# Weight pieces, output buffers and load order at the start of an attention and SwiGLU kernel

**Chip, cores, metric.** One core of one Trainium2 chip. The metric is the time of one execution on the device in microseconds (us). Where a ratio is quoted, it is the mean time of one kernel's fast runs over that of the other's fast runs of the same rounds, so not quite the ratio of the medians beside it.

## The reference

Softmax attention over 8 batches of 12 heads, 448 positions of 64 values; then the rows of all heads together (3584 x 768) go through a SwiGLU block of width 1536.

```
scores = q @ k^T / 8;  attn = softmax(scores);  x = (attn @ v)      # (8, 12, 448, 64)
x = x.transpose(0, 2, 1, 3).reshape(3584, 768)
g = x @ w_gate;  h = g * sigmoid(g) * (x @ w_val);  out = h @ w_out # (3584, 768) float32
```

## The kernel before

It works on pairs of heads. For each pair, TensorE turns q and k (`tp`) or, from pair 11 on, a DMA does; then come the scores `s`, the exponentials `E` on ScalarE, their sums and `pv` (tile `acc`). From pair 6 on, TensorE mixes the SwiGLU work of finished batches into the attention: `gp` and `vp` (gate and value, twelve column blocks each), then `op` (output). Until the first `gp` there is no SwiGLU work, and ScalarE's exponentials set the pace.

All loads of q, k, v and weights, except q and k of pair 0, are cast to 16 bits on the way. They go through one queue that GpSimd fills in program order. The parts that the change touches:

```python
WSPL = [(0, 384), (384, 384), (768, 768)]        # column pieces of gate and value
...
def load_w(kind, i): ...                          # each piece in two transfers, even and odd row pairs
...
def ffn2_steps(kk, c0, n, hts, first, last_block):        # op; first: block 0
    chunks = range(n // 128)
    if first:
        steps = [(ch, oh) for oh in range(2) for ch in chunks]    # all left halves, then all right
    else:
        steps = [(ch, oh) for ch in chunks for oh in range(2)]
    for ch, oh in steps:
        last = first or (last_block and ch == n // 128 - 1)
        if last or oh == 0:
            osb = fp.tile([128, DM], FP32, tag="osb", bufs=3)     # block 0: six tiles, half used
        ...                                       # 12 op matmuls into op
        nc.scalar.activation(osb[:, ds(m0, w)], op[:, 0:w], AF.Copy, scale=1.0 / HS)
        if not last:
            m0, w = 0, DM
            if oh == 0:
                continue                          # store whole chunks, except in block 0
        ...                                       # nc.sync.dma_start(out[...], osb[...])
...
load_qk16(1, 1); load_qk16(2, 1); load_qk16(3, 1)
load_v(0)                                         # v of pairs 0 to 2
load_qk16(4)                                      # q and k of pairs 4 and 5
load_v(1)
...
wq = {                                            # loads issued while pair number ... runs
    0: [("qk", 6), ("g", 0), ("v", 0)],
    1: [("qk", 8), ("g", 1), ("v", 1)],
    3: [("qk", 10), ("V", 2), ("g", 2), ("v", 2)],
    4: [("qk", 12)],
    6: [("V", 3), ("o", 0)],
    7: [("o", 1)],
}
```

The stores of the output and the DMA transposes share SyncE's queue, which is in order. Piece 2 of the value weights, used from column block 6 on, is called "value 2" below.

The softmax here doesn't subtract the row's maximum and nothing guards it: scores larger than these inputs give would overflow.

Of the kernel before, what the change touches and what calls it, by code (L numbers as in the profile page):

```python
# [10 lines left out]
FP32 = mybir.dt.float32  # L11
FP16 = mybir.dt.float16
# [15 lines left out]
def kernel(  # L28
# [10 lines left out]
    nc = tc.nc  # L39
    B, H, S, D = q.shape  # L40
    DM = H * D
    DF = moe_w_gate.shape[1]
    P = 112
    NC = S // P
    NCB = DM // 128
# [22 lines left out]
    consts = ctx.enter_context(tc.tile_pool(name="consts", bufs=1))  # L68
# [5 lines left out]
    fp = ctx.enter_context(tc.tile_pool(name="fp", bufs=3))  # L74
# [4 lines left out]
    ones = consts.tile([P, 32], FP16, name="ones")  # L79
    warm = consts.tile([128, 512], FP16, name="warm")  # L80
    ident = consts.tile([P, P], FP16, name="ident")
    WSPL = [(0, 384), (384, 384), (768, 768)]
    wgv = {}
    for kind in "gv":
        for i, (m0, m) in enumerate(WSPL):
            wgv[kind, i] = consts.tile([128, NCB, m], FP16, name=f"w{kind}{i}")

    def wslice(kind, fb, cb):
        i = min(fb // 3, 2)
        return wgv[kind, i][:, cb, ds(fb * 128 - WSPL[i][0], 128)]  # L90

    wo = [consts.tile([128, NFB, OH], FP16, name=f"wo{i}") for i in range(2)]

# [19 lines left out]
    def load_qk16(pr, n=2):  # L113
        q16 = raws.tile([P, 4, NC, D], FP16, tag="rq", bufs=RB, name="q16")
        k16 = raws.tile([P, 4, NC, D], FP16, tag="rk", bufs=RB, name="k16")
        for dst, src in ((q16, q), (k16, k)):
            flat = src.rearrange("b h s d -> (b h) s d")[2 * pr : 2 * pr + 2 * n]
            nc.gpsimd.dma_start(dst[:, 0 : 2 * n], flat.rearrange("h (p c) d -> p h (c d)", c=NC))
        for i in range(n):
            raw[pr + i] = (q16[:, 2 * i : 2 * i + 2], k16[:, 2 * i : 2 * i + 2])  # L120

    def load_v(g, lo=0, hi=2 * GP):
        b = g // GPB
        h0 = (g % GPB) * 2 * GP
        if lo == 0:
            v16[g] = raws.tile([P, 2 * GP, NC, D], FP16, tag="vt", bufs=3, name="vt")
        nc.gpsimd.dma_start(  # L127
            v16[g][:, lo:hi],
            v[b, h0 + lo : h0 + hi].rearrange("h (p c) d -> p h (c d)", c=NC),
        )  # L130

    def load_w(kind, i):
        if kind == "o":
            src = moe_w_out[:, ts(i, OH)].rearrange("(f p) m -> p f m", p=128)
            dst = wo[i]
        else:
            src = (moe_w_gate if kind == "g" else moe_w_val)[:, ds(*WSPL[i])].rearrange(
                "(a p t) m -> t p a m", p=128, t=2
            )
            for t in range(2):  # L140
                nc.gpsimd.dma_start(wgv[kind, i][:, t::2, :], src[t])
            return
        nc.gpsimd.dma_start(dst[:], src)
# [116 lines left out]
    def mm(dst, lhsT, rhs, start, stop):  # L260
        if not tiled[0]:
            nc.tensor.matmul(dst, lhsT=lhsT, rhs=rhs, start=start, stop=stop)  # L262
            return
        for j in range(4):
            nc.tensor.matmul(  # L265
                dst[ts(j, 32), :], lhsT=lhsT[:, ts(j, 32)], rhs=rhs, start=start, stop=stop
            )

    def ffn1_steps(kk, c0, n, hts):
        for fb in range(NFB):  # L270
            gp = ps_f.tile([128, 512], FP32, tag="f")
            for cb in range(NCB):
                mm(
                    gp[:, 0:n],
                    lhsT=wslice("g", fb, cb),
                    rhs=X[kk][:, cb, ds(c0, n)],
                    start=(cb == 0),
                    stop=(cb == NCB - 1),
                )
            sg = fp.tile([128, 512], FP32, tag="sg")  # L280
            nc.scalar.activation(sg[:, 0:n], gp[:, 0:n], AF.Tanh, scale=0.5)  # L281
            yield NCB * n / 2400.0
            vp = ps_f.tile([128, 512], FP32, tag="f")
            for cb in range(NCB):
                mm(
                    vp[:, 0:n],
                    lhsT=wslice("v", fb, cb),
                    rhs=X[kk][:, cb, ds(c0, n)],
                    start=(cb == 0),
                    stop=(cb == NCB - 1),  # L290
                )
            t1 = fp.tile([128, 512], FP32, tag="t1")
            nc.vector.scalar_tensor_tensor(  # L293
                t1[:, 0:n], sg[:, 0:n], 1.0, gp[:, 0:n], ALU.add, ALU.mult
            )
            nc.vector.scalar_tensor_tensor(  # L296
                hts[:, fb, 0:n], t1[:, 0:n], 0.5 * HS, vp[:, 0:n], ALU.mult, ALU.mult
            )
            yield NCB * n / 2400.0

    def ffn2_steps(kk, c0, n, hts, first, last_block):
        chunks = range(n // 128)
        if first:
            steps = [(ch, oh) for oh in range(2) for ch in chunks]
        else:
            steps = [(ch, oh) for ch in chunks for oh in range(2)]
        for ch, oh in steps:
            last = first or (last_block and ch == n // 128 - 1)
            if last or oh == 0:
                osb = fp.tile([128, DM], FP32, tag="osb", bufs=3)  # L310
            parts = [(oh * OH, OH)]
            if last_block and last and oh:
                parts = [(OH, OH // 2), (OH + OH // 2, OH // 2)]
            for m0, w in parts:
                op = ps_f.tile([128, 512], FP32, tag="f")
                for fb in range(NFB):
                    mm(
                        op[:, 0:w],
                        lhsT=hts[:, fb, ts(ch, 128)],
                        rhs=wo[oh][:, fb, ds(m0 - oh * OH, w)],  # L320
                        start=(fb == 0),
                        stop=(fb == NFB - 1),
# [5 lines that stand above are left out]
                        continue  # L328
                l0 = c0 + ch * 128
                l = l0  # L330
                while l < l0 + 128:
                    b, j = divmod(l, S)
                    c, p0 = divmod(j, P)
                    m = min(P - p0, l0 + 128 - l)
                    eng = nc.scalar if last_block and last and m < 64 else nc.sync
                    eng.dma_start(
                        out[ts(NB * kk + b, S), :].rearrange("(p c) m -> c p m", c=NC)[
                            c, p0 : p0 + m, ds(m0, w)
                        ],
                        osb[l - l0 : l - l0 + m, ds(m0, w)],  # L340
                    )
                    l += m
            yield NFB * OH / 2400.0

    def block(i):
        kk, odd = divmod(i, 2)
        c0, n = (384, 512) if odd else (0, 384)
        hts = hp_.tile([128, NFB, 512], FP16, tag="h")
        return ffn1_steps(kk, c0, n, hts), ffn2_steps(kk, c0, n, hts, i == 0, i == B - 1), n

    with tc.manual_schedule():
# [4 lines left out]
        make_identity(nc, ident)  # L356
        load_qk16(2, 1)
        load_qk16(3, 1)
        load_v(0)
        load_qk16(4)  # L360
        load_v(1)
        dummy(6)
        prep(0)()
# [4 lines left out]
            0: [("qk", 6), ("g", 0), ("v", 0)],  # L368
            1: [("qk", 8), ("g", 1), ("v", 1)],
            3: [("qk", 10), ("V", 2), ("g", 2), ("v", 2)],  # L370
            4: [("qk", 12)],
            6: [("V", 3), ("o", 0)],
            7: [("o", 1)],
        }
# [1 line left out]
        def emit(item):  # L376
            if item[0] == "qk":
                load_qk16(*item[1:])
            elif item[0] == "V":
                load_v(item[1])  # L380
            else:
                load_w(*item)
# [152 lines left out]
```

## Time and profile before

| | before |
|---|---|
| time, median of three runs (range) | 467.75 us (465.63 to 468.91) |
| span of the profiled run | 466.1 us |
| TensorE busy | 453.2 us, 97% |
| TensorE idle before 95 us, from 95 to 400, after 400 | 7.7, 0, 5 us |
| TensorE's wait for wv (the value weights) | 1.6 us |
| ScalarE's two waits for output stores in block 0 | 5.1 us together |

How to read it: TensorE has no hole for 305 us, so only what happens in the first 95 us and at the very end can move the time. The lines themselves stand in the prediction.

### The profile page before, as it was taken

How to read it: one execution, taken by the hardware profiler on the slowest of the kernel's cores; microseconds unless marked ns; L12 is line 12 of the kernel's file. 1: busy time of each engine (PE TensorE's matmuls, PEld its weight loads, DVE VectorE, ACT ScalarE, POOL GpSimd, SP SyncE). 2: the span in 40 equal slices, each digit the busy share in tenths (PEclk: the TensorE clock that was granted, in tenths of full speed). 3: DMA queues.
4: the chain of work that ended last, by engine and by line, in shares of the span. 5: the costliest groups of instructions: out<-in, count | busy, mean ns of one | idle time of the engine just before them, and what ended most of it. 6: DMA issues, size and time to landing. Idle time of an engine off the chain costs nothing.

```text
span 466.1 us, 14143 instructions
## 1 busy us (share of the span) xinstructions
PE 453.2 (97%) x6367; PEld 228.0 (49%) x6367; DVE 237.0 (51%) x371; ACT 242.9 (52%) x353; POOL 101.0 (22%) x160
## 2 busy tenths in 40 slices
PE   8799899999999999999999999999999999999995
PEld 3344444344455555444455555544445556555453
DVE  2665664366764553655545644636555546434310
ACT  7886555656565555545555565555555552222221
POOL 9454406331350042302223040210200000000000
PEclk9999999999999999999999999999999999999999
DMA  9999999991994383771948574913602111110123
GB/s 132 194 200 208 192 181 196 203 151 24 110 129 57 65 114 53 117 106 18 135 45 107 90 118 86 123 23 75 97 10 55 37 37 35 36 35 1 35 69 101
DMA packets 80925, 44.24 MB, mean 95 GB/s; under 512 B 36704, under 2 KB 77792, under 8 KB 80864
## 3 DMA queue, kind: packets, MB, share of 16 engines
q0 software_dynamic: 40768, 23.37, 38.6%
q1 hardware_dynamic: 40000, 19.92, 23.6%
q8 instruction: 50, 0.82, 0.7%
q14 instruction: 11, 0.09, 0.1%
q10 hardware_dynamic: 96, 0.05, 0.0%
HBM read 47.19 MB, written 11.01 MB: 125 GB/s over the span
## 4 chain that ended last, share of the span: by engine, by line
PE 80%; DMA 15%; POOL 2%; issue 1%; ACT 0%; SPq 0%; POOLq 0%; ACTq 0%
PE gp L265 14%; PE vp L265 12%; PE op L262 11%; PE op L265 10%; DMA q<-in_q_dram 9%; PE vp L262 9%; PE s L197 7%; PE acc L213 7%; PE gp L262 7%; PE acc L235 3%; DMA wg<-in_moe_w_gate_dram 3%; DMA k<-in_k_dram 2%; DMA out_dram<-osb 2%; POOL vt L127 0%; POOL qk L155 0%
## 5 line engine op out<-in xcount | busy, mean ns | idle before, releaser
L204 ACT ACTIVATE E<-s 112x896 f16<-112x896 f32 x192 | 164.8, 918 | 25.3 <-PE s L197 25.1
L281 ACT ACTIVATE sg<-gp 128x384 f32<-128x384 f32 (+1 forms) x96 | 52.3, 545 | 86.8 <-PE gp L265 54.2
L293 DVE SCALAR_TENSOR_TENSOR t<-sg,gp 128x384 f32<-128x384 f32 (+1 forms) x96 | 58.5, 610 | 64.9 <-ACT sg L281 64.8
L324 ACT ACTIVATE osb<-op 128x384 f32<-128x384 f32 (+1 forms) x57 | 27.7, 486 | 102.6 <-PE op L262 53.2
L265 PE MATMUL gp<-X,wg 128*32 128x512 f16 (+1 forms) x1416 | 78.1, 355 | 0.0
L250 DVE RECIPROCAL R<-ssb 128x112 f32<-128x112 f32 x92 | 73.1, 827 | 0.7
L296 DVE SCALAR_TENSOR_TENSOR hts<-t,vp 128x384 f16<-128x384 f32 (+1 forms) x96 | 59.6, 621 | 24.9 <-PE vp L262 8.4
L262 PE MATMUL op<-wo,hts 128*128 128x384 f16 (+1 forms) x408 | 68.6, 322 | 0.0
L265 PE MATMUL vp<-X,wv 128*32 128x512 f16 (+1 forms) x1224 | 66.9, 353 | 0.0
L227 DVE TENSOR_TENSOR X<-acc,R 128x448 f16<-128x448 f32 x48 | 29.7, 624 | 65.8 <-PE acc L213 64.0
L262 PE MATMUL vp<-X,wv 128*128 128x384 f16 (+1 forms) x270 | 58.6, 353 | 1.6 <-DMA wv<-in_moe_w_val_dram 1.6
L197 PE MATMUL s<-qkT 64*128 64x448 f16 x384 | 55.1, 355 | 3.4 <-ACT E L204 3.1
L262 PEld LDWEIGHTS <-hts 128*128 128x128 f16 x408 | 38.9, 98 | 28.2 <-issue 3.0
L265 PEld LDWEIGHTS <-wg 128*32 128x32 f16 x1416 | 37.8, 97 | 29.6
L265 PE MATMUL op<-wo,hts 128*32 128x384 f16 x1104 | 48.9, 326 | 0.0
L262 PE MATMUL gp<-X,wg 128*128 128x384 f16 (+1 forms) x222 | 47.4, 350 | 0.0
L265 PEld LDWEIGHTS <-wv 128*32 128x32 f16 x1224 | 32.7, 97 | 25.5
L213 PE MATMUL acc<-E,vt 112*32 112x448 f16 x768 | 45.2, 355 | 0.0
L127 POOL DMA_DIRECT2D vt<-in_v_dram x16 | 12.4, 774 | 148.1 <-PE acc L213 146.3
L262 PEld LDWEIGHTS <-wv 128*128 128x128 f16 x270 | 25.2, 98 | 28.6 <-issue 4.6
L265 PEld LDWEIGHTS <-hts 128*32 128x32 f16 x1104 | 29.5, 97 | 16.4
L155 POOL COPY qk<-q 112x512 f16<-112x512 f16 x37 | 22.9, 620 | 65.0 <-DMA qkT<-qk 46.2
(38 smaller groups left out, 198.6 us busy)
## 6 DMA issues: line engine op xcount, KB each, us to landing
vt<-in_v_dram POOLq DMA_DIRECT2D x16, 336.0 KB, 5.4
q<-in_q_dram POOLq DMA_DIRECT2D x22, 224.0 KB, 6.1
k<-in_k_dram POOLq DMA_DIRECT2D x22, 224.0 KB, 8.1
wo<-in_moe_w_out_dram POOLq DMA_DIRECT2D x2, 1152.0 KB, 26.1
out_dram<-osb SPq DMA_DIRECT2D x7, 288.0 KB, 2.8
out_dram<-osb SPq DMA_DIRECT2D x6, 336.0 KB, 2.9
out_dram<-osb SPq DMA_DIRECT2D x7, 240.0 KB, 2.7
out_dram<-osb SPq DMA_DIRECT2D x8, 192.0 KB, 2.7
```

The costliest lines, as they stand in the source:

```text
L155: nc.gpsimd.tensor_copy(dst, src)
L197: nc.tensor.matmul(s[:, hx, 0:S], lhsT=t[ts(hx, 64)].rearrange("p c q -> p (c q)")[:, c * P : c * P + 128], rhs=t[ts(hx, 64), NC:, :].rear ...
L204: nc.scalar.activation(E[pr][:, c], s[0:P, :, 0:S], AF.Exp, scale=sm_scale)
L213: nc.tensor.matmul(acc[ts(j, 32), 0:S], lhsT=v16[g][:, 2 * r + j % 2, c, :].rearrange("p (d t) -> p t d", t=2)[:, t], rhs=E[p0 + j // 2][: ...
L227: nc.vector.tensor_tensor(X[kk][:, hp + t, ts(bb, S)], acc[:, 0:S], R[p0][:], ALU.mult)
L250: lambda i=i: nc.vector.reciprocal(rt[:, ts(i, P)], ssb[:, ts(i, P)]) for i in range(4)
L262: nc.tensor.matmul(dst, lhsT=lhsT, rhs=rhs, start=start, stop=stop)
L265: nc.tensor.matmul(dst[ts(j, 32), :], lhsT=lhsT[:, ts(j, 32)], rhs=rhs, start=start, stop=stop)
L281: nc.scalar.activation(sg[:, 0:n], gp[:, 0:n], AF.Tanh, scale=0.5)
L293: nc.vector.scalar_tensor_tensor(t1[:, 0:n], sg[:, 0:n], 1.0, gp[:, 0:n], ALU.add, ALU.mult)
L296: nc.vector.scalar_tensor_tensor(hts[:, fb, 0:n], t1[:, 0:n], 0.5 * HS, vp[:, 0:n], ALU.mult, ALU.mult)
L324: nc.scalar.activation(osb[:, ds(m0, w)], op[:, 0:w], AF.Copy, scale=1.0 / HS)
```

## The change

Three intents: let the weights of column block 6 arrive sooner by moving fewer bytes ahead of them; give each output chunk of block 0 its own buffer for both halves, so that no eviction waits for a store; and have q and k of pairs 4 and 5 arrive sooner.

```diff
-    WSPL = [(0, 384), (384, 384), (768, 768)]
...
-        for i, (m0, m) in enumerate(WSPL):
-            wgv[kind, i] = consts.tile([128, NCB, m], FP16, name=f"w{kind}{i}")
+        for i in range(4):
+            wgv[kind, i] = consts.tile([128, NCB, DF // 4], FP16, name=f"w{kind}{i}")
...                                               (wslice and load_w follow suit)
+        osbs = {}
         for ch, oh in steps:
-            last = first or (last_block and ch == n // 128 - 1)
+            last = last_block and ch == n // 128 - 1
             if last or oh == 0:
-                osb = fp.tile([128, DM], FP32, tag="osb", bufs=3)
+                osbs[ch] = fp.tile([128, DM], FP32, tag="osb", bufs=3, name="osb")
+            osb = osbs[ch]
...
+        load_qk16(4)
         load_v(0)
-        load_qk16(4)
         load_v(1)
...
-            4: [("qk", 12)],
+            4: [("g", 3), ("v", 3), ("qk", 12)],
```

They are called part 1 (weights), part 2 (output) and part 3 (pairs).

## The prediction

> **What bounds the kernel now.** I read the page first, then the waits of TensorE, the TensorE timeline up to 135 us, and last the DMA landings and the waits of ScalarE and GpSimd. The page's first two parts:
>
> ```profile
> PE 453.2 (97%) x6367; PEld 228.0 (49%) x6367; DVE 237.0 (51%) x371; ACT 242.9 (52%) x353; POOL 101.0 (22%) x160
> ...
> PE   8799899999999999999999999999999999999995
> ...
> DMA  9999999991994383771948574913602111110123
> ```
>
> TensorE is busy in 97% of 466.1 us, so nothing that leaves its arithmetic alone can win more than the other 13 us. The change leaves it alone: same matmuls, shapes and order. Summed over windows, TensorE idles 7.7 us before 95 us, none from 95 to 400, and 5 us around the last store. A slice is 11.65 us, so the first nine slices of DMA, all at 9, say that its engines are full up to about 100 us. The holes in TensorE lie in the same stretch. The waits of TensorE, up to 30 us (first fence) and from 30 to 100 us (second):
>
> ```profile
> PE s L197 <- ACT E L204: 2.2, 5, 0.4
> ...
> PE tp L185 <- DMA k<-in_k_dram: 0.7, 1, 0.7
> ...
> PE tp L185 <- DMA q<-in_q_dram: 0.2, 1, 0.2
> ```
>
> ```profile
> PE vp L262 <- DMA wv<-in_moe_w_val_dram: 1.6, 1, 1.6
> PE s L197 <- ACT E L204: 0.9, 2, 0.4
> ```
>
> Each part of the diff aims at one of these: "pairs 4 and 5 sooner" at the first tp waits, the finer weight pieces at the wait for wv, and the three output buffers at the two waits for E after 30 us. Those two look like ScalarE's fault, but the waits of ScalarE between 60 and 100 us say why E is late:
>
> ```profile
> ACT osb L324 <- DMA out_dram<-osb: 5.1, 2, 2.7
> ```
>
> Block 0 makes six tiles of half an output chunk from a ring of three, so the fourth and the sixth eviction that count wait for a store to free its buffer (2.47 us at 80.78, 2.66 us at 87.54), and the exponentials behind them in ScalarE's order wait too. The page's chain of waits agrees: "DMA out_dram<-osb" holds 8.12 us from 79.32, and after 89.66 the chain is TensorE alone up to the final op matmuls at 443 us. **So a microsecond won before 90 us is a microsecond at the end.**
>
> **What the Trainium skill says.** "Perfetto Trace Analysis", Summary: the profiler window per engine type: for a GpSimd-issued DMA the profiler shows descriptor generation and hides the data movement. The trace agrees: such a load holds GpSimd 0.77 us and lands 10 to 28 us later, so landings are what count. "DMA: Bandwidth & Descriptors", Queues, rings and completion order: an engine takes descriptors of a ring in ring order, though completion is not first-in-first-out by rule. In this trace the landings of this queue do come in issue order (v of group 0 at 13.3, q of pair 4 at 14.5, its k at 15.6). The same page, Specifications, puts the line-rate minimum at 512 B. The new weight rows are 768 B in the fast memory instead of 1,536 B, above it; the trace shows 200 GB/s in windows where 768 B pieces move and 209 where 1,536 B pieces move. "Perfetto Trace Analysis", DMA Optimizations, says that splitting may help if DMA engines are generally idle. Here they are full, so I expect the gain from the changed order of bytes alone.
>
> **Part 1, weights in four pieces.** Pieces 0 and 1 were 384 columns already. Only the 768-column piece becomes two of 384, and gate 3 and value 3 now follow value 2. Four more issues of 0.77 us come on GpSimd, which is 22% busy: free. The TensorE timeline at the wait:
>
> ```profile
> 48.30 0.33 PE L262 MATMUL vp<-X,wv 128*128 128x384 f16 x1
> 50.22 0.99 PE L262 MATMUL vp<-X,wv 128*128 128x384 f16 x5 [1.59 <-DMA wv<-in_moe_w_val_dram]
> 51.04 1.14 PE L262 MATMUL gp<-X,wg 128*128 128x384 f16 x6
> ```
>
> The second half-transfer of value piece 2 was issued at 32.7 and landed 17.5 us later, at 50.2. From the first matmul here to the next group is 51.04 - 48.30 = 2.74 us; six such matmuls elsewhere start the next group after 0.98. Lost: **1.76 us**. After the change, half of gate 2 and half of value 2, 2 x 576 KB = 1.18 MB, leave the queue ahead of this landing; at 200 GB/s that is 5.9 us, so it lands at about 44.3, needed at 47.6 (part 3 wins 0.7 before). The wait goes with 3 us to spare. Gate 3 and value 3 land where all of piece 2 did, near 50, and are first used with column block 9, at 57.9 - 2.5 = 55. No wait.
>
> **Part 2, output of block 0.** Three whole-chunk tiles, one per chunk, are filled in both halves. Three buffers for three tiles: no eviction waits on a store. Six evictions remain; 12 stores become 6 with rows of 3,072 B, fewer issues on SyncE, which is no bound. What TensorE loses now:
>
> ```profile
> 82.13 0.37 PE L197 MATMUL s<-qkT 64*128 64x448 f16 x2
> 82.94 0.36 PE L197 MATMUL s<-qkT 64*128 64x448 f16 x2 [0.44 <-ACT E L204]
> 83.23 0.94 PE L213 MATMUL acc<-E,vt 112*32 112x448 f16 x16
> ```
>
> Undisturbed, four s matmuls start the next group 0.48 us after their own start (78.64 to 79.13). Here it is 1.10, and at 88.89 it is 1.11 (next group at 90.00). Lost: 0.62 + 0.63 = **1.25 us**, well below ScalarE's 5.1 us of waiting, because that engine has slack which soaks up the rest.
>
> **Part 3, pairs 4 and 5 before v of group 0.**
>
> ```profile
> 14.03 0.36 PE L197 MATMUL s<-qkT 64*128 64x448 f16 x2
> 14.57 0.39 PE L185 MATMUL tp<-ident,q 112*64 112x112 f16 x8 [0.17 <-DMA q<-in_q_dram]
> 15.67 0.39 PE L185 MATMUL tp<-ident,k 112*64 112x112 f16 x8 [0.71 <-DMA k<-in_k_dram]
> 15.99 0.36 PE L197 MATMUL s<-qkT 64*128 64x448 f16 x2
> 16.28 0.94 PE L213 MATMUL acc<-E,vt 112*32 112x448 f16 x16
> ```
>
> Undisturbed, the steps s, q transposes, k transposes, s take 0.30, 0.22, 0.30 us, as at 10.44 to 11.26. Then pv (the last line) would start at 14.03 + 0.30 + 0.22 + 0.30 + 0.29 = 15.14, not 16.28: at most 1.14 us. But now v of group 0 is behind 448 KB of q and k. The three transfers hold the same bytes in any order, so the last of them still lands near 15.6; formerly that was k, now it is v. pv waits from 15.14 to about 15.55 and wins **0.7 us**. q and k land about 1.7 us sooner (344 KB at some 200 GB/s), at 12.8 and 13.9, before the 14.33 and 14.55 at which they are wanted. ScalarE, full in this stretch, had 1.04 + 0.25 us of idleness behind the late s; with s at 14.85 and the next at about 16.4 its later exponentials start some 0.7 us sooner, so the win isn't lost again there.
>
> **Sum.** 1.76 + 1.25 + 0.7 = 3.7 us, all before the gapless stretch: 467.75 - 3.7 = **464.0 us**, 0.8% less.
>
> **Rivals.** (a) A later load becomes the wait. With TensorE 2.5 us earlier, the first op matmuls come at 64.8 instead of 67.2. GpSimd reuses one of eight completion slots per load (each issue of the weights waits for the landing of the one eight before it), so the w_out loads, issued at 38.4 and 41.9, will go out at about 44 and 46. They landed at 61.9 and 70.6 behind a full queue, and the bytes ahead of them stay the same, so I expect the same landings: 2.9 us of slack for the first, 3.5 for the second (wanted at 76.6 - 2.5 = 74.1). For this rival speaks only the smaller rows: 2.36 MB at 200 instead of 209 GB/s costs 0.5 us. If it came true, the total win would be about 2 us: 465.7. (b) v of group 0 lands later than I take it, say at 16.3: part 3 wins nothing, 464.7. If instead v streams faster behind q, k and pv doesn't wait, 463.6. (c) SyncE's in-order queue: the store of a chunk sits behind transposes which wait for late q and k (four issues there stretch from 44.1 to 74.7). It formerly passed that delay to ScalarE. With a buffer per chunk the next user of the ring is block 1 at 138 us, so this path is cut; were it not, part 2's 1.25 us would stay: 465.3. (d) Nothing shows, since all the gain is 0.8% and the three times of before spread by 0.7%; that is a matter of reading, not of the mechanism.
>
> **Range and chances.** The mechanism gives 463.4 to 465.7; the spread of the median of three adds about 1 us on either side. So 462.4 to 466.2. Over 2% faster would need 9.4 us, more than all the TensorE idleness before 95 us; over 2% slower would need a new hole of 13 us. Chances 0.01, 0.98, 0.01.
>
> **What the new profile should show.** Right: no TensorE wait for wv near 47; gate 3 and value 3 waited for by nobody; no wait of ScalarE's osb for out_dram; TensorE waits for E only before 30 us; the first pv waits a few tenths for v instead of tp for k; TensorE's busy time still 453, span about 462.4. Step by step, the first gp group (30.25 now) should be at 29.5, the first op group (67.23) at 64.8, and the first gp group of block 1 (87.41) at about 84.3. Wrong: a wait for wo before op, for qkT before an s near 62 or 84, or a pv that waits a microsecond or more.

## The result

The first comparison gave 462.47 us (462.01 to 463.61, four runs) against 467.56 us (465.63 to 468.91, four runs), ratio 0.9898, interval 0.9858 to 0.9938. A second one with more rounds (`after_again` below) gave 463.40 us against 466.15, ratio 0.9932, interval 0.9916 to 0.9948. Predicted were 464.0 us, 462.4 to 466.2, within 2%.

The page of the changed kernel, first parts:

```profile
PE 452.3 (98%) x6367; PEld 227.8 (49%) x6367; DVE 236.8 (51%) x371; ACT 243.0 (53%) x353; POOL 104.2 (23%) x164
...
PE   8899999999999999999999999999999999999996
...
DMA  9999999995793484662758393903603111100123
```

TensorE's busy time is the same within 1 us; the work did not change, the holes did. The DMA engines are as full as before for the same stretch. All waits of TensorE in the changed kernel (us in total, times, longest):

```profile
PE s L196 <- ACT E L203: 2.2, 5, 0.4
PE wp L103 <- DVE ones L355: 1.2, 1, 1.2
PE acc L234 <- ACT E L203: 0.4, 1, 0.4
PE s L196 <- DVE qkT L175: 0.2, 1, 0.2
```

No wait for a DMA is left, and none at all after 30 us. ScalarE between 60 and 100 us:

```profile
ACT osb L325 <- PE op L261: 7.9, 6, 2.3
```

Its six evictions of block 0 wait only for the matmuls, never for out_dram. The TensorE timeline where the three holes were:

```profile
14.35 0.39 PE L184 MATMUL tp<-ident,q 112*64 112x112 f16 x8
14.57 0.36 PE L184 MATMUL tp<-ident,k 112*64 112x112 f16 x8
14.87 0.36 PE L196 MATMUL s<-qkT 64*128 64x448 f16 x2
15.16 0.94 PE L212 MATMUL acc<-E,vt 112*32 112x448 f16 x16
...
47.18 1.14 PE L261 MATMUL vp<-X,wv 128*128 128x384 f16 x6
48.16 1.14 PE L261 MATMUL gp<-X,wg 128*128 128x384 f16 x6
...
79.17 0.55 PE L196 MATMUL s<-qkT 64*128 64x448 f16 x4
79.65 0.94 PE L212 MATMUL acc<-E,vt 112*32 112x448 f16 x16
```

The first pv starts at 15.16, not 16.28: 1.12 us won. The six vp matmuls of column block 6 take the ordinary 0.98 us to the next group, formerly 2.74: 1.76 us won. Four s matmuls take 0.48 us to the next group. From the first op (67.23, now 64.35) to the last block of 120 op matmuls (443.13, now 438.86) 375.90 us became 374.51: 1.39 us won. Sum **4.27 us**.

The two spans differ by 5.9 us, 1.6 more than that, and the 1.6 lies after the last op start: 22.97 us against 21.34. That part isn't the change's; see `before_again`.

### The profile page after: what moved, and what is told of

Same layout as the page of the kernel before. It is cut to its first block, busy times and chain, and to the rows that moved or that the text cites. A ratio compares the mean times of both kernels' runs of the same rounds, so it can differ in the third digit from the quotient of the medians.

```text
span 460.2 us, 14133 instructions
## 1 busy us (share of the span) xinstructions
PE 452.3 (98%) x6367; PEld 227.8 (49%) x6367; DVE 236.8 (51%) x371; ACT 243.0 (53%) x353; POOL 104.2 (23%) x164
## 4 chain that ended last, share of the span: by engine, by line
PE 95%; ACT 3%; DMA 1%; DVE 0%; issue 0%; SPq 0%; ACTq 0%
PE gp L264 15%; PE op L261 14%; PE vp L264 13%; PE vp L261 11%; PE op L264 10%; PE s L196 10%; PE gp L261 9%; PE acc L212 9%; PE acc L234 4%; ACT E L203 2%; DMA rk<-in_k_dram 1%; PE tp L184 1%; PE wp L103 0%; PE tp L167 0%; DVE qkT L175 0%
## 5 line engine op out<-in xcount | busy, mean ns | idle before, releaser
L264 PEld LDWEIGHTS <-hts 128*32 128x32 f16 x1104 | 29.5, 97 | 16.3
L154 POOL COPY qk<-q 112x512 f16<-112x512 f16 x37 | 22.9, 620 | 63.9 <-DMA qkT<-qk 46.4
```

The lines of the kernel that those rows point to most:

```text
L154: nc.gpsimd.tensor_copy(dst, src)
L264: nc.tensor.matmul(dst[ts(j, 32), :], lhsT=lhsT[:, ts(j, 32)], rhs=rhs, start=start, stop=stop)
```

## The experiments

**How they are read.** Single times spread by over 2 us, about as much as a part is worth. The traces are sharper, if each is cut at four marks on TensorE: the first gp, the first op, the start of the last 120 op matmuls, and the end. All runs in one table (us), the stretch called "front" running from the start to the first gp:

| kernel | first pv | front | gp to op | op to last op | last op start | tail | median time |
|---|---|---|---|---|---|---|---|
| before | 16.28 | 30.25 | 36.98 | 375.90 | 443.13 | 22.97 | 467.56 |
| before_again | 16.82 | 32.04 | 35.22 | 376.13 | 443.39 | 21.31 | 466.57 |
| weights_only | 16.22 | 30.19 | 35.21 | 380.72 | 446.12 | 21.28 | 469.02 |
| output_only | 17.91 | 32.98 | 35.21 | 374.51 | 442.70 | 22.90 | 466.62 |
| pairs_only | 16.51 | 30.48 | 37.63 | 375.20 | 443.31 | 21.29 | 466.27 |
| no_output | 15.72 | 29.70 | 35.21 | 380.37 | 445.28 | 21.22 | 468.76 |
| no_weights | 15.33 | 29.30 | 37.39 | 374.51 | 441.20 | 22.90 | 465.14 |
| no_pairs | 16.77 | 30.74 | 35.21 | 374.52 | 440.47 | 21.43 | 463.38 |
| value2_last | 16.56 | 30.53 | 35.96 | 374.51 | 441.00 | 21.40 | 464.25 |
| after | 15.16 | 29.13 | 35.22 | 374.51 | 438.86 | 21.34 | 462.47 |
| after_again | 15.36 | 29.33 | 35.22 | 374.51 | 439.06 | 21.34 | 463.40 |
| half_stores | 15.19 | 29.16 | 35.22 | 374.51 | 438.89 | 21.21 | 462.12 |
| v0_after_v1 | 17.03 | 32.23 | 35.21 | 374.52 | 441.96 | 21.34 | 464.97 |
| one_more_dma_turn | 16.59 | 30.55 | 34.80 | 374.51 | 439.86 | 21.34 | 462.85 |

The medians are of four runs each (six for after_again). Each later group of runs had its own runs of the kernel before, with medians from 466.15 to 466.64 us; the 467.56 in the table is from the first comparison. Each row rests on one trace, so its stretches show a single execution.

**The theories.** The prediction summed three independent wins. After comparing the two traces I held a second theory, of fixed landings: a wait for a DMA ends when the transfer lands, and where the DMA queue is full that moment doesn't move with TensorE. Then a microsecond won ahead of such a wait is lost in it, and the parts are worth something only together.

### Each part alone, and the pair without part 2

`weights_only` takes over the four pieces and the new queue entry, and nothing else:

```diff
-    WSPL = [(0, 384), (384, 384), (768, 768)]     # and its uses
+    ... four pieces of DF // 4
-            4: [("qk", 12)],
+            4: [("g", 3), ("v", 3), ("qk", 12)],
```

> Part 1 alone. Measure: start of the last block of 120 op matmuls on TensorE (443.13 us before, 438.86 after). Theory of fixed landings (formed from the two traces): the wait for wv at 48.3 goes and op starts 1.8 us sooner (65.5 for 67.2), but the stores of block 0 land when they did, since they wait behind loads of a full DMA queue, so ScalarE's wait for out_dram grows by as much as TensorE came sooner: last op start 442.9 to 443.2, nothing won. Rival, the sum of the prediction (each part wins its own): 1.76 us, last op start 441.4.

Measured: 469.02 us, ratio 1.0042 (1.0007 to 1.0077), a little **slower**. The wait for wv is gone (gp to op 35.21) and op starts at 65.40, as both theories said. Then everything is lost and more. ScalarE between 60 and 100 us:

```profile
ACT osb L323 <- DMA out_dram<-osb: 5.8, 2, 5.4
```

and TensorE behind it:

```profile
83.25 0.56 PE L196 MATMUL s<-qkT 64*128 64x448 f16 x2 [2.96 <-ACT E L203]
84.06 0.56 PE L196 MATMUL s<-qkT 64*128 64x448 f16 x2 [0.25 <-ACT E L203]
84.55 1.68 PE L212 MATMUL acc<-E,vt 112*32 112x448 f16 x16
86.16 3.75 PE L261 MATMUL op<-wo,hts 128*128 128x384 f16 x12
```

The fourth eviction, which waits for a store, ran at 81.90; in before_again it ran at 81.73. TensorE started its fourth op group, which leads to that wait, at 74.76 here and at 76.61 in before_again, and got nothing for being earlier. What I had not expected is the op group of 3.75 us, elsewhere 2.12. The stretches of the timeline (length, then busy time of TensorE and the other engines, the last three columns granted clock, DMA share, GB/s):

```profile
80.00:82.00 2.00, 0.29 (x2) 0.09 (x1) 0.00 (x0) 0.10 (x1) 1.28 (x2) 1.00 1.30 201
82.00:84.00 2.00, 0.56 (x2) 0.11 (x2) 0.00 (x0) 2.00 (x3) 0.00 (x0) 0.67 1.37 218
84.00:86.00 2.00, 1.94 (x18) 0.56 (x17) 0.00 (x0) 1.59 (x4) 0.00 (x0) 0.50 1.23 122
86.00:88.00 2.00, 2.00 (x10) 0.88 (x7) 0.62 (x1) 0.53 (x1) 0.64 (x2) 0.50 1.35 223
```

After the hole, TensorE runs at half its clock for between six and seven microseconds (the next stretch, 88 to 90 us, still reads 0.63). Between before_again and weights_only the eviction differs by 0.17 us and the last op start by 2.73; the half clock lies between them. It is not there in every run. By its runs, the time follows the mean granted clock: 467.39 us at 0.999, 468.89 at 0.996, 469.15 and 469.69 at 0.993.

The Trainium skill describes this in "TensorE: Matmul & The Clock Gate", Part 1, What's actually happening: an idle array falls to half its clock, judged over a free-running window of about 3.4 us, so the moment depends on where in the window the work falls. The clock of 0.50 here and the chance from run to run agree; but the hole before it was 2.96 us, shorter than that window (see the last section).

`output_only` takes over the `osbs` lines alone.

> Part 2 alone. Both theories: the wait for wv at 48.3 stays at 1.6 us, ScalarE's waits for out_dram go, 1.25 to 1.4 us won: last op start 441.7 to 441.9.

Measured: 466.62 us, ratio 0.9998 (0.9958 to 1.0039). By the stretches the expectation holds where it speaks of the change: op to last op is 374.51, 1.39 us less than before. The rest is the front, 2.7 us later than in before:

```profile
14.78 0.39 PE L185 MATMUL tp<-ident,q 112*64 112x112 f16 x8 [0.32 <-DMA q<-in_q_dram]
17.12 0.39 PE L185 MATMUL tp<-ident,k 112*64 112x112 f16 x8 [1.95 <-DMA k<-in_k_dram]
17.44 0.54 PE L197 MATMUL s<-qkT 64*128 64x448 f16 x2
17.91 1.68 PE L213 MATMUL acc<-E,vt 112*32 112x448 f16 x16
```

k of pairs 4 and 5 landed 1.5 us later than in the profile of before, and behind the hole the clock halves again (pv 1.68 us for 0.94). TensorE reached column block 6 so late that it no longer waited for wv at all; my expectation of 1.6 us missed that. The lateness of the front and the old wait for wv overlap. As a time this run is inconclusive; its runs at clock 1.0 and 0.999 took 465.36 and 465.82 us, those at 0.995 took 467.41 and 468.45.

`pairs_only` moves `load_qk16(4)` ahead of `load_v(0)` and no more.

> Part 3 alone. Fixed landings: the first pv starts at 15.2 for 16.3, but value piece 2 still lands near 50.2, so TensorE's wait for wv grows from 1.6 to about 2.7 us and nothing is won: op starts at 67.2, last op start 443.1. Rival, the sum: 0.7 to 1.1 us won, last op start 442.0 to 442.4.

Measured: 466.27 us, ratio 0.9989 (0.9956 to 1.0022), last op start 443.31: nothing won. No tp waits for q or k any more. In this run the first pv still started at 16.51, not 15.2, because TensorE's first matmuls stayed slow until about 10 us (see the last section), and value 2 landed at 51.10:

```profile
51.10 0.99 PE L262 MATMUL vp<-X,wv 128*128 128x384 f16 x5 [2.24 <-DMA wv<-in_moe_w_val_dram]
```

So this run is a weak test of the theory: nothing was won ahead of the wait (first gp at 30.48, before 30.25). `no_weights` below tests it better.

`no_output` is part 1 and part 3 without part 2.

> Parts 1 and 3 without part 2. Fixed landings: op starts at 64.4 as in the changed kernel, then ScalarE's waits for out_dram grow to about 5 us each or in sum by 2.9 us, and the last op start is 442.9 to 443.2: all 2.9 us given back. Rival, the sum: last op start 440.2.

Measured: 468.76 us, ratio 1.0030 (0.9975 to 1.0084). op starts at 64.91, 2.3 us sooner than in before, and the last op start is 445.28, **2.15 us later** than in before. The fourth eviction waited 6.00 us for its store and ran at 81.98; over the four kernels without part 2 (besides before) it ran at 81.66 to 81.98, and at 80.78 in before, while TensorE came to it at times from 74.26 to 77.47. So the moment at which these stores land does not move with TensorE. SyncE's queue in no_output shows why:

```profile
48.12 27.18 SPq L157 DMA_TRANSPOSE qkT<-qk  x4
75.36 2.81 SPq L335 DMA_DIRECT2D out_dram<-osb  x4
```

The first tile was evicted at 67.55, but its store was issued at 75.36 only. It stood behind a transpose, which waited for GpSimd's copies of q and k (from 72.30), and these for a load of q (16.25 us of waiting). The fourth eviction came 6.6 us after the issue. In the kernels with the old output code the first store was issued at 74.70 to 75.62 and the fourth eviction followed 6.1 to 6.6 us later, in every one. So "behind loads of a full DMA queue", as I expected, was half of it: the late loads reached the stores through SyncE's in-order queue, as rival (c) of the prediction has it. No run took the transposes out of the way, so how soon the stores would land without them is not shown.

Here too the clock halved: 3.15 us for the last op group of block 0. The run at clock 1.000 took 465.68 us, those at 0.993 took 469.20 and 469.75.

### One part left out, and the two other controls

`no_weights` is part 2 and part 3.

> Parts 2 and 3 without part 1. Fixed landings: wait for wv grows to about 2.7 us and swallows part 3; only part 2 counts, last op start 441.7 (1.4 us won). Rival, the sum: 2.5 us won, 440.6.

Measured: 465.14 us, ratio 0.9969 (0.9946 to 0.9992). The front is as good as in the changed kernel (29.30), and TensorE waits 2.00 us for wv; value 2 landed at 49.67. Of part 3 little is left: the last op start is 441.20, 1.93 us ahead of before, of which 1.39 are part 2 and 0.55 come from value 2 landing that much sooner in this run. Fixed landings said 441.7, the sum 440.6; the truth lies between. The first is a little nearer, and the wait grew, from 1.59 to 2.00 us, but not by all that part 3 had won.

`no_pairs` is part 1 and part 2.

> Parts 1 and 2 without part 3. Both theories: the first pv back at 16.3, no wait for wv and none for out_dram, 3.15 us won: last op start 440.0.

Measured: 463.38 us, ratio 0.9933 (0.9914 to 0.9953), last op start 440.47 against 440.0 expected. Both middle stretches are those of the changed kernel (35.21 and 374.52). The difference is the front: TensorE waited 0.5 us for q and 0.8 us for k of pair 4.

`value2_last` keeps all four pieces and changes their order:

```diff
-            3: [("qk", 10), ("V", 2), ("g", 2), ("v", 2)],
-            4: [("g", 3), ("v", 3), ("qk", 12)],
+            3: [("qk", 10), ("V", 2), ("g", 2), ("g", 3)],
+            4: [("v", 3), ("v", 2), ("qk", 12)],
```

> The changed kernel, same four pieces, but value piece 2 issued last of the four, so that as many bytes go ahead of it as before. If what helps is the bytes ahead: it lands near 50, TensorE arrives at 47.2 and waits some 2.7 us for it, last op start about 441.6. Rival, that finer pieces (smaller transfers or finer waits) help by themselves: no wait, last op start 438.9.

Measured: the wait is back, at a landing of 49.48 us:

```profile
49.48 0.99 PE L261 MATMUL vp<-X,wv 128*128 128x384 f16 x5 [0.57 <-DMA wv<-in_moe_w_val_dram]
```

It is 0.6 us and not 2.7 because the front of this run was 1.4 us late (the slow first matmuls again), so TensorE came at 48.58 and not at 47.18. In the changed kernel value 2 landed at 43.7 (its last transfer was issued at 32.66 and the profile gives 11.0 us to landing). So it is the bytes ahead that count, not the size of the pieces: same pieces, last in line, and the landing is 5.8 us later. The prediction reckoned 5.9 us for these bytes.

`before_again` is the kernel before, unchanged.

> The kernel before, unchanged. In the first pair of traces the span fell by 5.9 us while the last op start came only 4.27 us sooner: from there to the end it was 22.97 us before and 21.34 after. If that 1.6 us is spread from run to run: this trace has its last op start at 443.1 within 0.2 and a tail anywhere from 21 to 23 us. Rival, that the change shortens the end too: a tail of 22.9 to 23.0 again here, and 21.3 to 21.4 in all kernels with the change.

Measured: 466.57 us, ratio to the other runs of the same kernel 0.9993. Last op start 443.39, tail **21.31**, as in the changed kernel; so the 1.6 us at the end of the first pair of traces are not the change's. Over all 14 profiles the tail is 21.2 to 21.4 in eleven and 22.9 to 23.0 in three (before, output_only, no_weights). In just these three the page counts one transfer more on the instruction queue; before, then before_again:

```profile
q8 instruction: 50, 0.82, 0.7%
```

```profile
q8 instruction: 49, 0.80, 0.7%
```

and in the three SyncE waits about 3.1 us for the last stores instead of 1.4 to 1.5. Why the additional fetch comes in some runs isn't settled. It was seen in three of the five profiles with three weight pieces and in none of nine with four, and the code of the two differs in length, so I can't exclude that part 1 makes it rarer.

This trace also shows a coincidence in the kernel before: the front was 1.79 us later than in the first trace (a half clock around 19 us), and the last op start only 0.26 us. The wait for wv had swallowed the lateness. Fixed landings hide losses as well as gains.

### Why does part 2 help, and how close is part 3?

`half_stores` keeps a tile per chunk, and stores each half at once as before:

```diff
-                if not last:
+                if not (last or first):
                     m0, w = 0, DM
```

> The changed kernel, three held tiles, but each half of a chunk of block 0 stored as soon as it is evicted (12 stores of half rows, as before). If holding a buffer per chunk is what helps: no wait of ScalarE for out_dram, last op start 438.9. Rival, that fewer and longer stores help (less on the in-order SyncE queue): a wait for out_dram or for a transpose comes back and the last op start is 439.3 or later.

Measured: 462.12 us, ratio 0.9926 (0.9904 to 0.9947), last op start 438.89, the changed kernel's to 0.03 us. What helps is the buffer per chunk. Whole-chunk stores, fewer and longer, add nothing here.

`v0_after_v1` swaps `load_v(0)` and `load_v(1)` in the changed kernel.

> The changed kernel with v of group 1 loaded before v of group 0, so that 344 KB more go ahead of what the first pv needs. The prediction had v of group 0 land at 15.6, with pv waiting for it; the trace after shows no wait and pv at 15.16. If v of group 0 lands only just in time there, it now lands some 1.7 us later, near 16.5, and pv waits 1.1 to 1.7 us: last op start 440.0 to 440.5. Rival, that it has more than 1.7 us to spare: no wait, 438.9.

Measured: pv waited, and then the clock halved:

```profile
17.03 1.09 PE L212 MATMUL acc<-E,vt 112*32 112x448 f16 x16 [1.85 <-DMA vt<-in_v_dram]
...
18.91 1.69 PE L212 MATMUL acc<-E,vt 112*32 112x448 f16 x16
```

The second pv took 1.69 us, as in weights_only. The last op start is 441.96, 3.10 us later than in the changed kernel: 1.87 for pv's start and 1.23 more from pv to the first gp (15.20 us, 13.97 in the changed kernel). The expectation of 440.0 to 440.5 held the wait roughly and not the clock. By the profile, v of group 0 landed at 17.0 here and at 14.7 in the changed kernel, 0.4 us before pv wanted it. In no_output, with the load order of the changed kernel, it landed at 15.7: pv waited 0.3 us and started at 15.72. Over the eight traces with that order the landing lies between 14.6 and 15.7.

### A step further, and a repeat

`one_more_dma_turn` is the changed kernel with `NPE = 10`: pair 10 is turned by a DMA transpose, not by TensorE.

> The changed kernel with pair 10 too turned by a DMA transpose, not by TensorE: 16 transposes fewer, 0.52 us of TensorE by its timeline. If no new wait comes: last op start 438.35, too little for the clock to tell from the changed kernel. Rival: 229 KB more in the full DMA queue make w_out land about 1.1 us later, after 64.35, and op waits: 438.9 or later; or the transposed tile is late for its first s near 59.5.

Measured: 462.85 us, in the same group as half_stores' 462.12. gp to op fell to 34.80, 0.42 us less, and no new wait came; but the front was one of the late ones (30.55). By the clock it is not better than the changed kernel.

`after_again` is the changed kernel, unchanged, with more rounds.

> The changed kernel, unchanged, with more rounds. Reading of the runs so far: the kernel falls into four stretches. From the first gp to the first op 35.21 us and from the first op to the last block of op 374.51 us, both without a hole and the same in every run; the start of the first gp varies with the chip's start (29.1, or about 30.5 where the first matmuls stay slow until 10 us), and the tail is 21.3 or 22.9 us. If that holds: 35.21 and 374.51 again to 0.05 us, first gp at 29.1 to 30.6, time 461.8 to 463.8, 0.7 to 1.0% below the kernel before. Rival, that the changed kernel too has waits for loads in some of its runs: one of the two middle stretches is longer by 0.3 us or more.

Measured: 35.22 and 374.51, front 29.33, tail 21.34; 463.40 us (461.95 to 463.81). The two middle stretches don't move by more than 0.02 us. Its runs fall into 461.95 to 462.26 and 463.37 to 463.81, so some chance is left. For three of the four slower runs the span is longer too (461.6 to 461.8 us, against 460.2 and 460.5 in the faster two), which leaves the front or the tail. The fourth, at 463.37, is the one with the trace; its span is 460.4, so its extra time lies outside the traced span.

## Why the prediction was right

The time was in the range at both comparisons, and the ratio of the larger one (0.9932) is 3.2 us of the mean, the prediction 3.7. Step by step:

- **Part 1.** Predicted 1.76 us, landing of value 2 at 44.3. Measured 1.76 us, landing at 43.7. Gate 3 and value 3 were waited for by nobody. The bytes ahead were the right quantity (value2_last).
- **Part 2.** Predicted 1.25 us, measured 1.39. The term was mis-sized a little: I read each hole from the start of the first s matmuls, and missed that these already started 0.07 us late, twice.
- **Part 3.** Predicted 0.7 us with pv waiting for v until 15.55; in the first trace 1.12 us, no wait. This is the good branch of rival (b), v streaming faster. The prediction took it that the last of the three transfers lands at the same moment in any order; it landed at 15.6 to 17.1 in the five traces with the old order (k last) and at 14.6 to 15.7 in the eight with the new one (v last). Why isn't settled. That pv did not wait was luck in part, as no_output shows.
- **Rival (a),** a wait for w_out, did not come true; w_out was issued at 44.8 and 45.8, as said, and op never waited for it. Its first half landed at 62.9, though, not at 61.9, which left 1.5 us of slack before the first op (64.35) and not 2.9. Rival (c) was cut by part 2, as said.
- **Sum.** 4.27 us on TensorE for 3.7. The marks named beforehand came a little sooner too: first gp 29.13 for 29.5, first op 64.35 for 64.8, first gp of block 1 83.83 for 84.3. Two slips changed nothing: GpSimd's loads land from 3.8 us after issue (v of group 0 after 7.5), not from 10, and the best of the prediction's own cases gives 463.6, not 463.4.
- **A sentence that was wrong:** "So a microsecond won before 90 us is a microsecond at the end." It holds in the changed kernel, where no wait for a landing is left. In the kernel before, the waits for value 2 and for the stores of block 0 stand behind the front; weights_only and no_output started op 1.8 and 2.3 us sooner and the last op block 3.0 and 2.2 us later than before (the half clock included). The profile of before could have told: the chain of waits, of which the prediction quotes the end, runs from 7.30 to 87.44 us through loads, GpSimd, SyncE and a store, and holds 0.41 us of TensorE, at 15.67; the wait for wv is not in it. My sum came out right because the change removes those waits together, which the prediction does not say. I treated the parts as independent, and they are not: without part 2 the other two were worth nothing in no_output, and without part 1 the wait for wv took nearly half of what part 3 won (0.95 us at the first gp, 0.54 at the first op). Besides, the part left out can cost more than its own term: without part 2 the last op start is 6.4 us later than in the changed kernel, and the term is 1.4.
- **Not foreseen at all:** the clock. A hole can cost as much again, or nearly, by the half clock behind it (1.87 us and 1.23 more in v0_after_v1), and it comes by chance.

The 5.1 us between the first medians are not all explained by the change: 4.27 are on TensorE's path in that pair of traces, and the profile of before also had the long tail.

## What to carry to other kernels

Before adding up wins, follow each one to the end and ask at each later wait whether the thing waited for moves too; a transfer in a full queue does not, nor does one issued from an in-order queue behind something that waits for such a transfer. Remove the last of such waits first, or all of them together. When parts of a change are as small as the spread of the times, cut the traces at fixed marks and compare stretches: here two of four stretches repeat to 0.02 us, and all the chance lies in the other two.

## What the Trainium skill lacked or had wrong

- "TensorE: Matmul & The Clock Gate", Why this matters for your kernels, advises no idle gaps over about 3 us between bursts. Here the clock halved behind a single hole of 1.85 us (v0_after_v1), and in before_again behind two of 0.67 and 0.75 us within 1.8 us, in a stretch in which TensorE was also partly idle before. In no_pairs holes of 0.47 and 0.77 us in the same place did not do it. So staying under 3 us is not enough; whether short holes add up, or where they fall in the window decides, these runs don't tell apart.
- The same page, Part 1, What you observe, lets the warm-up vary by half a microsecond (further on it calls it run-variable). Here, in three of 14 profiles (pairs_only, value2_last, one_more_dma_turn), the first matmuls stayed slow (0.61 us for a lone 512-column one, elsewhere 0.39) until about 10 us, elsewhere only until about 5, and the front came 1.4 us later. The granted clock in those stretches reads 1.00 all the same, so this column does not show the slow start. That this is the same gate is my reading, and not shown.
- No page says that the end of a program can take 21.3 or 22.9 us after the same mark, with one more transfer of the instruction queue in the longer case.
- "DMA: Bandwidth & Descriptors" gives single transfers their time by size; for a full queue of casting loads what was needed was the rate at which the queue drains, about 200 GB/s of 16-bit data here. By it the landing of value 2 was foretold to 0.6 us (44.3, measured 43.7), that of v of group 0 to 0.9 us (15.55, measured 14.7).
